# A planned attention kernel: VectorE's two PSUM banks used one by one, batches of two, half of the int16 shifts moved to GpSimd

## The chip, the cores and the metric

One core of a Trainium2 chip runs the kernel. The metric is the device time in microseconds (us). Runs are compared in the state "fast" alone; the one slow run, of `e_fill65`, is marked where its profile is used. The span is the time from the first to the last instruction in a profile, about 2 us shorter than the device time. In the profile DVE is VectorE, ACT is ScalarE, POOL is GpSimd, PE is TensorE's matmuls and PEld its weight loads.

## The reference

Two attention blocks over the same input (2048 tokens, width 512, 32 heads of 16), mixed by a gate. Block A is softmax attention and takes nearly all the time; block B is linear attention.

```python
qkv = (x @ wqkv).reshape(B, S, 3, H, Dh) ...         # S = 2048, H = 32, Dh = 16
scores = jnp.einsum("bhqd,bhkd->bhqk", q, k) * (Dh ** -0.5)
p = _softmax(scores, axis=-1)
o = jnp.einsum("bhqk,bhkd->bhqd", p, v)              # A; then @ wo
...                                                   # B: linear attention with phi
return g * a + (1 - g) * b
```

## The kernel before

The scores are 2048 *units* of 128 x 512. TensorE writes a unit into a bank of PSUM (the "S" matmuls; the tile `ps` in the profile). Each unit is exponentiated in one of two ways.

- **ScalarE**: one `Exp` for two units (two banks).
- **VectorE**: a *conversion* adds a constant to the scaled scores and writes them as int16, so that the bits read as a bf16 number are roughly an exponential. Two *shifts* add 43 and 86 to those integers. The three results, with three scalings of the values, add up to a good exponential, so such a unit costs three value ("PV") matmuls instead of one.

The whole order of work is planned in Python when the kernel is built. Where the plan leaves a gap on TensorE, and its work in the last 3413 ns of planned time is below the share `FILL`, the planner puts in *fills*: matmuls on a dummy tile (`warm`).

```python
def d_choose(start, late=0.0):                 # units for VectorE: both banks (4 and 5) or none
    if d_busy[0] or max(t_free(4), t_free(5)) > max(start + 30.0, late):
        return []
    ...
    return [(cur, j, u, 4 + k) for k, (j, u) in enumerate(got)]

def cand_op1():                                # the conversion, of two banks at once
    ...
    return C(DV, 400, 533 * n + 74, lambda: nc.vector.tensor_scalar(o, i, ZB, 0.0, op0=ALU.add, op1=ALU.max), ...)

def cand_shift():                              # a batch is four units: 2048 int16 values
    ...
    return C(DV, 300, 602, lambda: nc.vector.tensor_scalar(Z[:, z, :], Z[:, z0, :], float(m), None, op0=ALU.add), ...)

while True:                                    # the planner
    ...
    for f in (cand_s, cand_dsolo, cand_pv, cand_op1, cand_shift, cand_exp):
    ...
    fin = emit(c.E, c.dur, c.fns, c.reads, c.writes, name=c.name)
```

The softmax here doesn't subtract the row's maximum and nothing guards it: scores larger than these inputs give would overflow.

Of the kernel before, what the change touches and what calls it, by code (L numbers as in the profile page):

```python
# [14 lines left out]
STATS = {}  # L15
# [110 lines left out]
def bass_gated_mix__mha_block__linear_attn_block__prompt_kernel(  # L126
# [31 lines left out]
    FILL = 0.65  # L158
    SLK = 0.0
# [3 lines left out]
    NPS, NZ, NQZ, NVQ = 10, 8, 3, 6  # L163

    with ExitStack() as es:
# [27 lines left out]
        ones = SB([128, 2], BF16, "ones")  # L193
        dummy = SB([128, 2], FP32, "dummy")
# [5 lines left out]
        Z = SB([128, NZ, 2048], I16, "Z")  # L200
# [58 lines left out]
        r_outt = [R(f"outt{i}") for i in range(2)]  # L259
        r_gt, r_ge, r_gl, r_gnat = R("gt"), R("ge"), R("gl"), R("gnat")  # L260
# [127 lines left out]
        emit(DV, 1000, lambda: nc.vector.memset(Vc[:, 0], 1.0), writes=r_V)  # L388
        emit(PO, 150, lambda: nc.gpsimd.memset(ones[:], 1.0), writes=[r_ones])
# [36 lines left out]
        d_busy = [False]  # L426
# [71 lines left out]
        def d_batch():  # L498

            if dst["cur"] is None:  # L500
                free = [z for z in range(NZ) if not z_pend[z]]
                if len(free) < NTERM + len(dst["shifts"]) + (NTERM - 1) * dst["open"]:
                    return None
                if all(d_unit(j) is None for j in range(4)):
                    return None
                z = min(free, key=lambda q: max([0.0] + list(r_Z[q].tr.values())))
                z_pend[z] = 1
                dst["open"] += 1
                dst["cur"] = {"todo": [0, 1, 2, 3], "z": z, "units": {}, "done": 0}
            return dst["cur"]  # L510

        def d_choose(start, late=0.0):

            if d_busy[0] or max(t_free(4), t_free(5)) > max(start + 30.0, late):
                return []
            cur = d_batch()
            if cur is None:
                return []
            js = sorted(cur["todo"], key=lambda j: (head(j), -len(uq[min(head(j), NR - 1)][j])))
            got = [(j, d_unit(j)) for j in js]  # L520
            got = sorted([x for x in got if x[1] is not None][:2])
            return [(cur, j, u, 4 + k) for k, (j, u) in enumerate(got)]
# [5 lines left out]
        class C:  # L528
            __slots__ = ("E", "prio", "dur", "fns", "reads", "writes", "after", "name", "mode", "wt")

            def __init__(self, E, prio, dur, fns, reads, writes, after, name, mode=None, wt=1.0):
                self.wt = wt
                self.E, self.prio, self.dur, self.fns = E, prio, dur, fns
                self.reads, self.writes, self.after, self.name, self.mode = reads, writes, after, name, mode

        def d_loaded(extra):
            for cur, j, u, bk in extra:
                r, kb = u
                take(r, kb, j)
                cur["todo"].remove(j)  # L540
                cur["units"][j] = u
                left[r][j] += NTERM - 1
                kb_left[(r, kb)] += NTERM - 1
            if extra:
                d_busy[0] = True
                dst["op1"].append((cur, [x[1] for x in extra]))
                if not cur["todo"]:
                    dst["cur"] = None

        def cand_s():  # L550
            sset = st["set"]
            if set_busy[sset]:
                return None
            b0 = 2 * sset
            writes = [r_bank[b0], r_bank[b0 + 1]]
            start = max(PE.free, _avail(PE, [], writes))
            extra = d_choose(start, s_window()[1] - SLK)
            units = act_pick(2, {x[1] for x in extra})
            if units is None and extra:
                extra = []  # L560
                units = act_pick(2, set())
            if units is None:
                return None
            n = len(units)
            reads = s_reads(units + [(u[0], u[1], j) for _, j, u, _ in extra])
            fns = [s_fn(r, kb, j, b0 + k) for k, (r, kb, j) in enumerate(units)]
            fns += [s_fn(u[0], u[1], j, bk) for _, j, u, bk in extra]
            writes = writes[:n] + [r_bank[x[3]] for x in extra]

            def after(fin):  # L570
                for (r, kb, j) in units:
                    take(r, kb, j)
                set_busy[sset] = True
                nn = n + 10 * len(extra)
                STATS["sn"][nn] = STATS["sn"].get(nn, 0) + 1
                exps.append((sset, units))
                st["set"] = 1 - sset
                d_loaded(extra)
            STATS.setdefault('sn', {})
            return C(PE, 1000, 222, fns, reads, writes, after, f"S{units}" + "".join(f"+D{x[2]}{x[1]}" for x in extra), "row",  # L580
                     0.25 * (n + len(extra)))
# [15 lines left out]
        def cand_op1():  # L597
            if not dst["op1"]:
                return None
            cur, js = dst["op1"][0]  # L600
            z = cur["z"]
            n = len(js)

            def after(fin):
                dst["op1"].popleft()
                d_busy[0] = False
                cur["done"] += n
                d_finish(cur)
            zj = Z[:, z, :].rearrange("p (j c) -> p j c", j=4)
            o = zj[:, js[0]:js[1] + 1:js[1] - js[0], :] if n == 2 else zj[:, js[0], :]  # L610
            i = bank(4, 2).rearrange("p (j c) -> p j c", j=2) if n == 2 else bank(4)
            return C(DV, 400, 533 * n + 74, lambda: nc.vector.tensor_scalar(o, i, ZB, 0.0, op0=ALU.add, op1=ALU.max),  # L612
                     [r_bank[4 + k] for k in range(n)], [r_Z[z]], after, f"op1 {[cur['units'][j] + (j,) for j in js]}")

        def z_items(cur, z, term):
            for j, (r, kb) in cur["units"].items():
                def rel():
                    z_pend[z] -= 1
                add_item(r, kb, j, Z[:, z, 512 * j:512 * (j + 1)].bitcast(BF16), r_Z[z], rel, term, f"z{term}")

        def d_finish(cur):
            n = len(cur["units"])
            if cur["done"] < n or (cur["todo"] and any(d_unit(j) is not None for j in cur["todo"])) or cur.get("fin"):
                return
            if cur["todo"]:
                if any(head(j) < NR - 1 for j in cur["todo"]):
                    return
                dst["cur"] = None
            cur["fin"] = True
            z = cur["z"]  # L630
            dst["open"] -= 1
            z_pend[z] = n + NTERM - 1
            z_items(cur, z, 0)
            for k, m in enumerate(SHIFTS[1:]):
                dst["shifts"].append((cur, m, z, k + 1))

        def cand_shift():
# [10 lines left out]
            cur, m, z0, kt = dst["shifts"][0]  # L648

            def after(fin):  # L650
                dst["shifts"].popleft()
                z_pend[z] = len(cur["units"])
                z_pend[z0] -= 1
                z_items(cur, z, kt)
            return C(DV, 300, 602, lambda: nc.vector.tensor_scalar(Z[:, z, :], Z[:, z0, :], float(m), None, op0=ALU.add),  # L655
                     [r_Z[z0]], [r_Z[z]], after, f"shift {m}")
# [205 lines left out]
        def t_v(t8, vb):  # L862
# [12 lines left out]
            for k in range(1, NTERM):  # L875
                yield po(750, lambda k=k: nc.gpsimd.tensor_scalar(Vc[:, k, vs].rearrange("p a b c -> p (a b c)"),  # L876
# [27 lines left out]
        def aout(r):  # L904
# [27 lines left out]
            yield po(800, lambda: nc.gpsimd.tensor_tensor(t2[:, :, 16 * par:16 * par + 16], t1[:, :, 0:16],  # L932
# [7 lines left out]
        def phi(b, dst_ap, dst_res):  # L940
# [6 lines left out]
            yield po(700, lambda: nc.gpsimd.tensor_scalar(eb[:, i, :], eb[:, i, :], 1.0, 0.0, op0=ALU.min, op1=ALU.max), [r_eb[i]], [r_eb[i]])  # L947
# [260 lines left out]
        def fill_one(start, mode):  # L1208
# [19 lines left out]
            free = [7] + [b for b in owner if owner[b] is None] + ([] if d_busy[0] or 4 in owner else [5, 4])  # L1228
# [20 lines left out]
        guard = 0  # L1249
        while True:  # L1250
# [7 lines left out]
            for f in (cand_s, cand_dsolo, cand_pv, cand_op1, cand_shift, cand_exp):  # L1258
                c = f()
                if c is not None:  # L1260
                    cands.append(c)
# [6 lines left out]
            for c in cands:  # L1268
                a = _avail(c.E, c.reads, c.writes)
                start0 = start = max(c.E.free, a)  # L1270
                if c.E is PE and c.mode and c.mode != st["mode"]:
                    start = max(start, PE.free + SWITCH)
                if c.E is PE and c.prio < 1000:
# [6 lines left out]
            key, start, c = min(by.values(), key=lambda v: v[1])  # L1280
            if c.E is PE:
# [9 lines left out]
                WLOG.append(act_log[-1])  # L1291
            if isinstance(c.fns, tuple) and c.fns[0] == "DMA":
# [72 lines left out]
```

## Time and profile before

| | before |
|---|---|
| median | 740.31 us (739.58 to 740.9, 3 runs) |
| units on ScalarE / VectorE | 1460 / 588 |
| busy: PE, VectorE, ScalarE, GpSimd | 93%, 90%, 94%, 17% |

First the engine line of the page: busy us, share of the span, number of instructions. Then groups of instructions: line, engine, operation, out<-in, shapes and count; busy us and mean ns of one; idle time of the engine just before them and what ended it. L677 are the exps, L612 the conversions, L655 the shifts.

```profile
PE 689.5 (93%) x6663; PEld 209.2 (28%) x6757; DVE 667.6 (90%) x813; ACT 697.7 (94%) x769; POOL 128.3 (17%) x184
...
L677 ACT ACTIVATE P<-ps 128x1024 bf16<-128x1024 f32 x730 | 682.4, 1045 | 23.3 <-PE ps L331 22.1
L612 DVE TENSOR_SCALAR Z<-ps 128x1024 int16<-128x1024 f32 x294 | 357.2, 1215 | 42.8 <-PE ps L331 41.8
...
L655 DVE TENSOR_SCALAR Z<-Z 128x2048 int16<-128x2048 int16 x294 | 215.4, 750 | 3.0
```

Three engines are above 90%, and GpSimd is nearly idle. ScalarE's exps plus the idle time in front of them make 682.4 + 23.3 = 705.7 us (a sum) of the 740.2 us span: ScalarE sets the pace, and only fewer exps or less waiting of ScalarE can shorten the run.

The next lines are of the timeline (start us, us, engine, line, operation), the first of GpSimd, the others of VectorE, in the same stretch.

```profile
229.04 1.27 POOL L948 TENSOR_TENSOR phiK<-eb,mb 128x512 bf16<-128x512 f32 x1
```
```profile
229.34 2.11 DVE L655 TENSOR_SCALAR Z<-Z 128x2048 int16<-128x2048 int16 x2
231.38 1.21 DVE L612 TENSOR_SCALAR Z<-ps 128x1024 int16<-128x1024 f32 x1
```

Two shifts, which elsewhere take 1.3 us together, took 2.11 us here; the first started while GpSimd was in an add and ended 0.55 us after it.

### The profile page before, as it was taken

How to read it: one execution, taken by the hardware profiler on the slowest of the kernel's cores; microseconds unless marked ns; L12 is line 12 of the kernel's file. 1: busy time of each engine (PE TensorE's matmuls, PEld its weight loads, DVE VectorE, ACT ScalarE, POOL GpSimd, SP SyncE). 2: the span in 40 equal slices, each digit the busy share in tenths (PEclk: the TensorE clock that was granted, in tenths of full speed). 3: DMA queues.
4: the chain of work that ended last, by engine and by line, in shares of the span. 5: the costliest groups of instructions: out<-in, count | busy, mean ns of one | idle time of the engine just before them, and what ended most of it. 6: DMA issues, size and time to landing. Idle time of an engine off the chain costs nothing.

```text
span 740.2 us, 16623 instructions
## 1 busy us (share of the span) xinstructions
PE 689.5 (93%) x6663; PEld 209.2 (28%) x6757; DVE 667.6 (90%) x813; ACT 697.7 (94%) x769; POOL 128.3 (17%) x184
## 2 busy tenths in 40 slices
PE   6999999899999999999999999999899989999997
PEld 2322222222323222222233322222233222222222
DVE  6799999998999999988897999999999968999894
ACT  4899999999999999999999999999999969999993
POOL 1301341212311220000010034233430000000000
PEclk8999999999999999999999999999999869999999
DMA  5900000000000000000000000000002021000001
GB/s 128 317 13 15 2 5 4 2 8 2 1 8 3 8 1 2 8 2 8 1 8 3 7 3 3 7 1 3 1 8 44 19 48 30 16 15 16 16 15 36
DMA packets 27836, 15.49 MB, mean 21 GB/s; under 512 B 19696, under 2 KB 26736, under 8 KB 27760
## 3 DMA queue, kind: packets, MB, share of 16 engines
q1 hardware_dynamic: 26704, 14.17, 7.0%
q8 instruction: 53, 0.87, 0.5%
q10 hardware_dynamic: 1056, 0.26, 0.2%
q14 instruction: 23, 0.19, 0.1%
HBM read 6.69 MB, written 2.10 MB: 12 GB/s over the span
## 4 chain that ended last, share of the span: by engine, by line
PE 58%; DVE 23%; ACT 9%; issue 7%; POOL 1%; DMA 0%; ACTq 0%; POOLq 0%; DVEq 0%
PE ps L331 58%; DVE Z L612 12%; ACT P L677 9%; DVE Z L655 6%; DVE mb L945 1%; DVE T L909 1%; DVE Vc L873 1%; DMA xnat<-wA 0%; DVE QT L845 0%; DVE OAT L936 0%; DVE KT L823 0%; ACT eb L944 0%; DVE wA L1032 0%; POOL Vc L876 0%; POOL phiK L948 0%
## 5 line engine op out<-in xcount | busy, mean ns | idle before, releaser
L677 ACT ACTIVATE P<-ps 128x1024 bf16<-128x1024 f32 x730 | 682.4, 1045 | 23.3 <-PE ps L331 22.1
L612 DVE TENSOR_SCALAR Z<-ps 128x1024 int16<-128x1024 f32 x294 | 357.2, 1215 | 42.8 <-PE ps L331 41.8
L331 PE MATMUL ps<-Qz,KT 32*128 32x512 bf16 x2048 | 291.3, 390 | 15.4 <-DVE Z L612 5.2
L331 PE MATMUL ps<-Z,Vc 128*17 128x512 bf16 x1764 | 227.8, 387 | 6.9 <-DVE Z L655 6.2
L655 DVE TENSOR_SCALAR Z<-Z 128x2048 int16<-128x2048 int16 x294 | 215.4, 750 | 3.0
L331 PE MATMUL ps<-P,Vc 128*17 128x512 bf16 x1460 | 204.0, 388 | 2.7 <-ACT P L677 0.9
L331 PEld LDWEIGHTS ps<-Qz,KT 32*128 32x128 bf16 x2048 | 73.7, 91 | 259.5 <-ACT P L677 182.5
L331 PEld LDWEIGHTS ps<-Z,Vc 128*17 128x17 bf16 x1764 | 52.1, 88 | 90.3 <-issue 45.2
L331 PE MATMUL ps<-warm 128*32 128x512 bf16 (+17 forms) x524 | 70.6, 334 | 3.8 <-issue 2.2
L331 PEld LDWEIGHTS ps<-P,Vc 128*17 128x17 bf16 x1460 | 47.3, 88 | 72.5 <-issue 35.4
L929 POOL TENSOR_TENSOR rg<-rec,gt 128x16 f32<-128x16 f32 x31 | 11.8, 380 | 297.2 <-DVE rec L916 297.2
L947 POOL TENSOR_SCALAR eb<-eb 128x512 f32<-128x512 f32 x32 | 23.1, 722 | 148.9 <-DVE mb L945 74.8
L948 POOL TENSOR_TENSOR phiK<-eb,mb 128x512 bf16<-128x512 f32 x32 | 43.2, 1350 | 2.3
L876 POOL TENSOR_SCALAR Vc<-Vc 128x576 bf16<-128x576 bf16 x32 | 23.3, 727 | 88.6 <-DVE Vc L873 87.3
L331 PE MATMUL ps<-xT,wA 128*128 128x512 bf16 x105 | 33.5, 388 | 5.1 <-issue 3.1
L909 DVE STREAM_TRANSPOSE T<-ps 128x512 f32<-128x512 f32 x32 | 22.6, 707 | 9.3 <-PE ps L331 9.3
L331 PEld LDWEIGHTS ps<-warm 128*32 128x32 bf16 (+1 forms) x541 | 20.6, 95 | 23.9 <-issue 17.9
L945 DVE TENSOR_SCALAR mb<-ps 128x512 f32<-128x512 f32 x32 | 21.6, 677 | 1.3 <-PE ps L331 0.9
L331 PE MATMUL ps<-wA,xT 128*128 128x128 bf16 x256 | 21.8, 226 | 0.6 <-DVE KT L823 0.2
L944 ACT ACTIVATE eb<-ps 128x512 f32<-128x512 f32 x32 | 20.0, 624 | 0.6 <-PE ps L331 0.6
L932 POOL TENSOR_TENSOR T<-T,rg 128x256 bf16<-128x256 f32 x31 | 19.6, 632 | 2.4
L331 PE MATMUL ps<-woA,OAT 128*128 128x512 bf16 x55 | 16.6, 382 | 2.2 <-DVE OAT L924 1.2
(76 smaller groups left out, 247.0 us busy)
## 6 DMA issues: line engine op xcount, KB each, us to landing
Qz<-QT SPq DMA_DIRECT2D x120, 16.0 KB, 1.8
wA<-in_A_wqkv_dram SPq DMA_DIRECT2D x1, 1536.0 KB, 8.4
wB<-in_B_wqkv_dram SPq DMA_DIRECT2D x1, 1536.0 KB, 11.8
xnat<-in_A_x_dram SPq DMA_DIRECT2D x3, 512.0 KB, 12.7
out_dram<-outt SPq DMA_DIRECT2D x12, 128.0 KB, 1.7
xnat<-in_A_x_dram SPq DMA_DIRECT2D x4, 128.0 KB, 3.3
woA<-in_A_wo_dram SPq DMA_DIRECT2D x1, 512.0 KB, 8.7
woB<-in_B_wo_dram SPq DMA_DIRECT2D x1, 512.0 KB, 9.3
```

The costliest lines, as they stand in the source:

```text
L331: return lambda: nc.tensor.matmul(o, lhsT=l, rhs=r, start=start, stop=stop, skip_group_check=sg)
L612: return C(DV, 400, 533 * n + 74, lambda: nc.vector.tensor_scalar(o, i, ZB, 0.0, op0=ALU.add, op1=ALU.max), [r_bank[4 + k] for k in range( ...
L655: return C(DV, 300, 602, lambda: nc.vector.tensor_scalar(Z[:, z, :], Z[:, z0, :], float(m), None, op0=ALU.add), [r_Z[z0]], [r_Z[z]], after ...
L677: return C(AC, 500, 427 * n + 49, lambda: nc.scalar.activation(P[:, slot, 0:512 * n], bank(b0, n), ACT.Exp, scale=ESC), [r_bank[b0 + k] fo ...
L876: yield po(750, lambda k=k: nc.gpsimd.tensor_scalar(Vc[:, k, vs].rearrange("p a b c -> p (a b c)"), Vc[:, 0, vs].rearrange("p a b c -> p ( ...
L909: yield dv(607, lambda: nc.vector.transpose(T1[:, a, :], bank(7)), [r_bank[7]], [r_T1[a]])
L929: yield po(250, lambda: nc.gpsimd.tensor_tensor(rg[:, a, :], rec[:, a, :], gt[:, qc, :], ALU.mult), [r_rec[a], r_gt], [r_rg[a]])
L932: yield po(800, lambda: nc.gpsimd.tensor_tensor(t2[:, :, 16 * par:16 * par + 16], t1[:, :, 0:16], rg[:, a, :].unsqueeze(2).to_broadcast([1 ...
L944: yield ac(480, lambda: nc.scalar.activation(eb[:, i, :], bank(b), ACT.Exp), [r_bank[b]], [r_eb[i]])
L945: yield dv(607, lambda: nc.vector.tensor_scalar(mb[:, i, :], bank(b), 0.0, 1e-6, op0=ALU.max, op1=ALU.add), [r_bank[b], r_eb[i]], [r_mb[i]])
L947: yield po(700, lambda: nc.gpsimd.tensor_scalar(eb[:, i, :], eb[:, i, :], 1.0, 0.0, op0=ALU.min, op1=ALU.max), [r_eb[i]], [r_eb[i]])
L948: yield po(1300, lambda: nc.gpsimd.tensor_tensor(dst_ap, eb[:, i, :], mb[:, i, :], ALU.add), [r_eb[i], r_mb[i]], dst_res)
```

## The change

The intent: (1) TensorE may refill one of VectorE's two banks while the other is being converted; (2) batches of two units, so that shifts come in smaller pieces; (3) roughly half of the shifts go to the idle GpSimd, two int16 values packed in one int32 add (if the add is exact, no carry crosses from the lower value, since the sums stay below 32768). VectorE then has room for more units, which come off ScalarE. The planner also keeps a GpSimd instruction and a VectorE shift apart in its planned times (`lock`, `port`; *port* is its name for the entry that does so). The ground for it is in the trace of before: of the 45 shifts that began while a GpSimd instruction ran, 44 ended after it (by 0.55 us at the median), and the longest took 1.75 us, where a free one takes 0.685. The threshold `FILL` rises from 0.65 to 0.75 as well. The core of it, with cuts inside lines and between them shown as `...`:

```diff
-    FILL = 0.65
-    SLK = 0.0
+    FILL = 0.75
...
+    PMIN = 2
...
+    SLK = 120.0
...
-    NPS, NZ, NQZ, NVQ = 10, 8, 3, 6
+    NB = 2
+    NPS, NZ, NQZ, NVQ = 10, 16, 3, 6
...
-            if d_busy[0] or max(t_free(4), t_free(5)) > max(start + 30.0, late):
+            banks = [b for b in (4, 5) if not d_busy[b] and t_free(b) <= max(start + 30.0, late)]
+            if not banks:
                 return []
...
+            if E is PO:
+                return C(PO, 400, 200 + 532 * n, lambda: nc.gpsimd.tensor_tensor(
+                    Z[:, z, 0:512 * n].bitcast(I32), Z[:, z0, 0:512 * n].bitcast(I32),
+                    mcon[:, kt - 1:kt].to_broadcast([128, 256 * n]), ALU.add), ...)
-            return C(DV, 300, 602, lambda: nc.vector.tensor_scalar(Z[:, z, :], Z[:, z0, :], float(m), ...
+            return C(DV, 450 if hot else 300, 69 + 134 * n, lambda: nc.vector.tensor_scalar(Z[:, z, 0:512 * n], ..., lock=True)
...
+                if c.lock:
+                    start = max(start, port["pool" if c.E is DV else "dve"])
...
+            if c.lock:
+                c.E.free = max(c.E.free, start)
+                port[c.E.name] = start + c.dur + 20.0
```

Left out: bookkeeping per bank, a few priorities and planned durations of other GpSimd work.

More of the change, by code (lines that the diff above doesn't have):

```diff
@@ L157, in bass_gated_mix__mha_block__linear_attn_block__prompt_kernel @@
     SWITCH = 100.0
-    FILL = 0.65
-    SLK = 0.0
+    FILL = 0.75
+    HOT = 24
+    BACK = 600.0
+    SHB = 2
+    why = [None]
+    PMIN = 2
+    PLATE = 0.0
+    SLK = 120.0
     DSL = 300.0
     STICK = 450.0
-    NPS, NZ, NQZ, NVQ = 10, 8, 3, 6
+    NB = 2
+    NPS, NZ, NQZ, NVQ = 10, 16, 3, 6
     with ExitStack() as es:
@@ L193, in bass_gated_mix__mha_block__linear_attn_block__prompt_kernel @@
         ones = SB([128, 2], BF16, "ones")
+        mcon = SB([128, 2], I32, "mcon")
         dummy = SB([128, 2], FP32, "dummy")
@@ L199, in bass_gated_mix__mha_block__linear_attn_block__prompt_kernel @@
         P = SB([128, NPS, 1024], BF16, "P")
-        Z = SB([128, NZ, 2048], I16, "Z")
+        Z = SB([128, NZ, 512 * NB], I16, "Z")
         T1 = SB([128, 2, 512], FP32, "T1")
@@ L259, in bass_gated_mix__mha_block__linear_attn_block__prompt_kernel @@
         r_outt = [R(f"outt{i}") for i in range(2)]
+        r_mcon = R("mcon")
         r_gt, r_ge, r_gl, r_gnat = R("gt"), R("ge"), R("gl"), R("gnat")
@@ L388, in bass_gated_mix__mha_block__linear_attn_block__prompt_kernel @@
         emit(DV, 1000, lambda: nc.vector.memset(Vc[:, 0], 1.0), writes=r_V)
+        for k, m in enumerate(SHIFTS[1:]):
+            emit(PO, 150, lambda k=k, m=m: nc.gpsimd.memset(mcon[:, k:k + 1], m * 65537), writes=[r_mcon])
         emit(PO, 150, lambda: nc.gpsimd.memset(ones[:], 1.0), writes=[r_ones])
@@ L425, in bass_gated_mix__mha_block__linear_attn_block__prompt_kernel @@
         owner = {6: None}
-        d_busy = [False]
+        dcnt = [[0] * 4 for _ in range(NR)]
+        d_busy = {4: False, 5: False}
         kb_left = {(r, kb): 4 for r in range(NR) for kb in range(NKB)}
@@ L508, in d_batch @@
                 dst["open"] += 1
-                dst["cur"] = {"todo": [0, 1, 2, 3], "z": z, "units": {}, "done": 0}
+                dst["cur"] = {"todo": NB, "z": z, "units": [], "done": 0}
             return dst["cur"]
         def d_choose(start, late=0.0):
-            if d_busy[0] or max(t_free(4), t_free(5)) > max(start + 30.0, late):
+            banks = [b for b in (4, 5) if not d_busy[b] and t_free(b) <= max(start + 30.0, late)]
+            if not banks:
+                why[0] = "busy" if any(d_busy[b] for b in (4, 5)) else "late"
                 return []
@@ L517, in d_choose @@
             if cur is None:
+                why[0] = "noZ"
                 return []
-            js = sorted(cur["todo"], key=lambda j: (head(j), -len(uq[min(head(j), NR - 1)][j])))
-            got = [(j, d_unit(j)) for j in js]
-            got = sorted([x for x in got if x[1] is not None][:2])
-            return [(cur, j, u, 4 + k) for k, (j, u) in enumerate(got)]
+            got = [(j, d_unit(j)) for j in range(4)]
+            got = sorted([x for x in got if x[1] is not None], key=lambda x: (x[1][0], dcnt[x[1][0]][x[0]], -len(uq[x[1][0]][x[0]])))
+            got = sorted(got[:min(len(banks) if len(dst["op1"]) < 1 and DV.free < start + BACK and len(dst["shifts"]) < SHB else 1, cur["todo"])])
+            why[0] = "none" if not got else "ok"
+            return [(cur, j, u, b) for b, (j, u) in zip(banks, got)]
         def add_item(r, kb, j, ap, res, rel, term, name):
@@ L528, in bass_gated_mix__mha_block__linear_attn_block__prompt_kernel, with __init__ @@
         class C:
-            __slots__ = ("E", "prio", "dur", "fns", "reads", "writes", "after", "name", "mode", "wt")
-            def __init__(self, E, prio, dur, fns, reads, writes, after, name, mode=None, wt=1.0):
+            __slots__ = ("E", "prio", "dur", "fns", "reads", "writes", "after", "name", "mode", "wt", "lock")
+            def __init__(self, E, prio, dur, fns, reads, writes, after, name, mode=None, wt=1.0, lock=False):
                 self.wt = wt
+                self.lock = lock or E is PO
                 self.E, self.prio, self.dur, self.fns = E, prio, dur, fns
@@ L539, in d_loaded @@
                 take(r, kb, j)
-                cur["todo"].remove(j)
-                cur["units"][j] = u
+                cur["todo"] -= 1
+                cur["units"].append((r, kb, j))
+                dcnt[r][j] += 1
                 left[r][j] += NTERM - 1
@@ L544, in d_loaded @@
             if extra:
-                d_busy[0] = True
-                dst["op1"].append((cur, [x[1] for x in extra]))
+                for x in extra:
+                    d_busy[x[3]] = True
+                for k, x in enumerate(extra):
+                    dst["op1"].append((cur, len(cur["units"]) - len(extra) + k, [x[3]]))
                 if not cur["todo"]:
@@ L557, in cand_s @@
             extra = d_choose(start, s_window()[1] - SLK)
+            w = why[0]
             units = act_pick(2, {x[1] for x in extra})
@@ L575, in after @@
                 STATS["sn"][nn] = STATS["sn"].get(nn, 0) + 1
+                STATS.setdefault("why", {})
+                STATS["why"][w] = STATS["why"].get(w, 0) + 1
                 exps.append((sset, units))
@@ L599, in cand_op1, with z_items @@
                 return None
-            cur, js = dst["op1"][0]
+            cur, k0, bks = dst["op1"][0]
             z = cur["z"]
-            n = len(js)
+            n = len(bks)
             def after(fin):
                 dst["op1"].popleft()
-                d_busy[0] = False
+                for b in bks:
+                    d_busy[b] = False
+                z_items(cur, z, 0, range(k0, k0 + n))
+                z_pend[z] += n
                 cur["done"] += n
                 d_finish(cur)
-            zj = Z[:, z, :].rearrange("p (j c) -> p j c", j=4)
-            o = zj[:, js[0]:js[1] + 1:js[1] - js[0], :] if n == 2 else zj[:, js[0], :]
-            i = bank(4, 2).rearrange("p (j c) -> p j c", j=2) if n == 2 else bank(4)
+            o = Z[:, z, 512 * k0:512 * (k0 + n)]
+            i = bank(bks[0], n)
             return C(DV, 400, 533 * n + 74, lambda: nc.vector.tensor_scalar(o, i, ZB, 0.0, op0=ALU.add, op1=ALU.max),
-                     [r_bank[4 + k] for k in range(n)], [r_Z[z]], after, f"op1 {[cur['units'][j] + (j,) for j in js]}")
-        def z_items(cur, z, term):
-            for j, (r, kb) in cur["units"].items():
+                     [r_bank[b] for b in bks], [r_Z[z]], after, f"op1 {cur['units'][k0:k0 + n]}")
+        def z_items(cur, z, term, ks):
+            for k in ks:
+                r, kb, j = cur["units"][k]
                 def rel():
                     z_pend[z] -= 1
-                add_item(r, kb, j, Z[:, z, 512 * j:512 * (j + 1)].bitcast(BF16), r_Z[z], rel, term, f"z{term}")
+                add_item(r, kb, j, Z[:, z, 512 * k:512 * (k + 1)].bitcast(BF16), r_Z[z], rel, term, f"z{term}")
         def d_finish(cur):
             n = len(cur["units"])
-            if cur["done"] < n or (cur["todo"] and any(d_unit(j) is not None for j in cur["todo"])) or cur.get("fin"):
+            if cur["done"] < n or (cur["todo"] and any(d_unit(j) is not None for j in range(4))) or cur.get("fin"):
                 return
             if cur["todo"]:
-                if any(head(j) < NR - 1 for j in cur["todo"]):
+                if any(head(j) < NR - 1 for j in range(4)):
                     return
@@ L631, in d_finish, with cand_pshift, cand_shift @@
             dst["open"] -= 1
-            z_pend[z] = n + NTERM - 1
-            z_items(cur, z, 0)
+            z_pend[z] += NTERM - 2
             for k, m in enumerate(SHIFTS[1:]):
                 dst["shifts"].append((cur, m, z, k + 1))
-        def cand_shift():
+        def cand_pshift():
+            return cand_shift(PO)
+        def cand_shift(E=DV):
             if dst["cur"] is not None and dst["cur"]["todo"]:
@@ L648, in cand_shift @@
             cur, m, z0, kt = dst["shifts"][0]
+            n = len(cur["units"])
+            if E is PO and (len(dst["shifts"]) < PMIN or PO.free > DV.free + PLATE):
+                return None
             def after(fin):
@@ L653, in after @@
                 z_pend[z0] -= 1
-                z_items(cur, z, kt)
-            return C(DV, 300, 602, lambda: nc.vector.tensor_scalar(Z[:, z, :], Z[:, z0, :], float(m), None, op0=ALU.add),
-                     [r_Z[z0]], [r_Z[z]], after, f"shift {m}")
+                z_items(cur, z, kt, range(len(cur["units"])))
+                STATS["sh" + E.name] = STATS.get("sh" + E.name, 0) + 1
+            if E is PO:
+                return C(PO, 400, 200 + 532 * n, lambda: nc.gpsimd.tensor_tensor(
+                    Z[:, z, 0:512 * n].bitcast(I32), Z[:, z0, 0:512 * n].bitcast(I32),
+                    mcon[:, kt - 1:kt].to_broadcast([128, 256 * n]), ALU.add), [r_Z[z0], r_mcon], [r_Z[z]], after, f"pshift {m}")
+            pr = st["pv_round"]
+            hot = pr < NR and sum(left[pr]) < HOT and any(u[0] <= pr for u in cur["units"])
+            return C(DV, 450 if hot else 300, 69 + 134 * n, lambda: nc.vector.tensor_scalar(Z[:, z, 0:512 * n], Z[:, z0, 0:512 * n], float(m), None, op0=ALU.add),
+                     [r_Z[z0]], [r_Z[z]], after, f"shift {m}", lock=True)
         def cand_exp():
@@ L875, in t_v @@
             for k in range(1, NTERM):
-                yield po(750, lambda k=k: nc.gpsimd.tensor_scalar(Vc[:, k, vs].rearrange("p a b c -> p (a b c)"),
+                yield po(690, lambda k=k: nc.gpsimd.tensor_scalar(Vc[:, k, vs].rearrange("p a b c -> p (a b c)"),
                                                                   Vc[:, 0, vs].rearrange("p a b c -> p (a b c)"), COEF[k], 1.0,
@@ L931, in aout @@
             t2 = T2[:, c, :].rearrange("p (q d) -> p q d", d=32)
-            yield po(800, lambda: nc.gpsimd.tensor_tensor(t2[:, :, 16 * par:16 * par + 16], t1[:, :, 0:16],
+            yield po(640, lambda: nc.gpsimd.tensor_tensor(t2[:, :, 16 * par:16 * par + 16], t1[:, :, 0:16],
                                                           rg[:, a, :].unsqueeze(2).to_broadcast([128, 16, 16]), ALU.mult),
@@ L946, in phi @@
             yield ("FREE", b)
-            yield po(700, lambda: nc.gpsimd.tensor_scalar(eb[:, i, :], eb[:, i, :], 1.0, 0.0, op0=ALU.min, op1=ALU.max), [r_eb[i]], [r_eb[i]])
+            yield po(640, lambda: nc.gpsimd.tensor_scalar(eb[:, i, :], eb[:, i, :], 1.0, 0.0, op0=ALU.min, op1=ALU.max), [r_eb[i]], [r_eb[i]])
             yield po(1300, lambda: nc.gpsimd.tensor_tensor(dst_ap, eb[:, i, :], mb[:, i, :], ALU.add), [r_eb[i], r_mb[i]], dst_res)
@@ L1227, in fill_one @@
             t0 = PE.free + (SWITCH if m == "row" else 0.0)
-            free = [7] + [b for b in owner if owner[b] is None] + ([] if d_busy[0] or 4 in owner else [5, 4])
+            free = [7] + [b for b in owner if owner[b] is None] + [b for b in (5, 4) if b not in owner and not d_busy[b]]
             free = [b for b in free if _avail(PE, [], [r_bank[b]]) <= t0]
@@ L1249, in bass_gated_mix__mha_block__linear_attn_block__prompt_kernel @@
         guard = 0
+        port = {"pool": 0.0, "dve": 0.0}
         while True:
@@ L1257, in bass_gated_mix__mha_block__linear_attn_block__prompt_kernel @@
             cands = cand_tasks()
-            for f in (cand_s, cand_dsolo, cand_pv, cand_op1, cand_shift, cand_exp):
+            for f in (cand_s, cand_dsolo, cand_pv, cand_op1, cand_shift, cand_pshift, cand_exp):
                 c = f()
@@ L1272, in bass_gated_mix__mha_block__linear_attn_block__prompt_kernel @@
                     start = max(start, PE.free + SWITCH)
+                if c.lock:
+                    start = max(start, port["pool" if c.E is DV else "dve"])
+                    start0 = max(start0, start)
                 if c.E is PE and c.prio < 1000:
@@ L1279, in bass_gated_mix__mha_block__linear_attn_block__prompt_kernel @@
                     by[c.E] = (key, start, c)
-            key, start, c = min(by.values(), key=lambda v: v[1])
+            key, start, c = min(by.values(), key=lambda v: v[1] - (80.0 if v[2].E is DV and v[2].lock else 0.0))
             if c.E is PE:
```

## The prediction

> **What bounds the kernel now.** Three engines are nearly full: in the table of windows, from 200 to 500 us, ScalarE is busy 99%, TensorE 95%, VectorE 93%. GpSimd is busy 17% over the span. The 2048 softmax units (128 x 512 scores) are shared out: 730 ScalarE exps and 294 VectorE conversions (group L612) take two each. In the timeline fourteen exps in a row take 13.27 us, 0.474 us a unit; ScalarE's time is 1460 x 0.474 = 692 us plus 48. The span falls only if units leave ScalarE, and VectorE decides how many can. In the timeline a conversion of a pair occupies VectorE 1.14 us, a shift of four units 0.61 us: 0.875 us a unit, 514 us. Its other 226 us are other work (about 90), start and tail, waits, and shifts blocked by GpSimd (group L655: mean 750, median 685, worst 1754 ns). The list of waits gives 41.8 us of L612 on TensorE: both banks are taken and freed together, so VectorE can stand still while a new pair is written.
>
> **What changes.**
> - Conversions bank by bank: TensorE refills one bank while the other is read. A 128x512 PSUM read of the same kind takes 0.60 us back to back, instead of 0.57 a unit: about +20 us, against perhaps 25 of the 42 us of waits.
> - [...] With half on GpSimd VectorE keeps 0.17 us a unit; in all 0.77, 12% less.
> - GpSimd gets some 300 int32 adds of 512 values. The like in the trace is the phi add (L948), 1269 ns median: about 0.4 ms more, 70-75% busy. [...]
> - [...] shifts starting during a GpSimd add take up to 1754 ns. GpSimd work plus VectorE shifts must fit one after the other: about 530 + 110 us of 715. It fits, tightly; conversions from PSUM can run beside GpSimd. I allow 15 us more blocking.
> - TensorE: about 55 more VectorE units are 110 more value matmuls, four at a time, some 6 us, plus more warm-up fills. No new bound, but little slack.
>
> **The sum.** ScalarE: (2048 - n) x 0.474 + 48. VectorE: n x 0.77 + 218 (226, less 25 of waits, plus 15 blocking, plus 2). Equal at n = 643: 714 us. The order of work is fixed beforehand and more engines now depend on each other: I add 3 us. Nearly all of the gain is on the critical path; some 30 us at start and tail stay.
>
> Prediction: 717 us (3.1% less), 8 in 10 between 698 and 735. Faster by over 2%: 0.68; within 2%: 0.26; slower: 0.06.
>
> **What would show it.** Exps fall from 730 to about 703, ScalarE still 98-99% busy in the middle; about 640 one-bank conversions; 300-340 VectorE shifts of 0.34-0.45 us; GpSimd 70-75% busy, adds of about 1.27 us; L612's wait on TensorE below 20 us.
>
> **What would make it wrong.** The port: if VectorE's shifts (mean far over 0.45 us) or the GpSimd adds stretch waiting for one another, the gain is eaten and the time stays at 735 or more. TensorE: if single-bank loads cost extra passes, or fills delay real work, ScalarE idles. If GpSimd's late terms hold up value matmuls, buffers run out. In the other direction, if nearly all waits vanish, 700 us.

The 0.17 us a unit rests on that estimate, so the sum can't be followed in full from what is printed: with 0.17, and so 0.77, taken as they stand it came to 714 us, and with the 3 us added to 717. The estimate was the author's; in the changed kernel free shifts of 1024 values start every 0.336 us in a row, and half of that is 0.17. What the other steps rest on in the trace of before: that GpSimd's work and the shifts must fit one after the other, on the 44 of 45 shifts above; that conversions can run beside GpSimd, on 79 of the 294 that overlap its instructions, of which the longest took 1225 ns, and of the others 1226; the 6 us of TensorE, on value matmuls in a row, four of which take 0.22 us (median, start to start).

## More of the kernel before

The runs were made in several sessions on different chips, each beside the kernel before, which had a median of 740.2 to 741.8 us in them; so times of two sessions are compared to about 2 us. The granted clock is the share of full clock that the profiler saw TensorE get.

The planner keeps for each engine the time when it is free, takes durations from written constants, picks the instruction that can start first, and emits it. What comes out is one fixed instruction stream per engine, with semaphore waits **only where data or buffers require them**. The planned times themselves are not in the program.

## The result, and the profile after

The changed kernel takes 748.56 us (748.27 to 752.29, 4 runs) against 740.21 us for before (4 runs). The ratio is 1.0124, 95% interval 1.0091 to 1.0157: within 2%, but on the slow side. (A ratio here is the mean time of one kernel's fast runs over that of the other's of the same rounds, so it is not quite the ratio of the medians.) The prediction of 717 us was wrong.

The same parts of the page of the changed kernel. L716 are the exps, L637 the conversions, L689 the GpSimd adds, L694 the VectorE shifts.

```profile
PE 685.4 (92%) x6934; PEld 211.8 (28%) x7026; DVE 672.6 (90%) x1131; ACT 691.2 (93%) x754; POOL 464.0 (62%) x519
...
L716 ACT ACTIVATE P<-ps 128x1024 bf16<-128x1024 f32 x715 | 675.7, 1037 | 36.1 <-PE ps L340 33.5
L637 DVE TENSOR_SCALAR Z<-ps 128x512 int16<-128x512 f32 x619 | 414.1, 682 | 48.7 <-PE ps L340 34.9
L689 POOL TENSOR_TENSOR Z<-Z,mcon 128x512 int32<-128x512 int32 x333 | 350.3, 1075 | 151.8 <-DVE Z L637 113.6
...
L694 DVE TENSOR_SCALAR Z<-Z 128x1024 int16<-128x1024 int16 (+1 forms) x287 | 168.4, 622 | 0.3
```

The work was moved as intended: 619 units on VectorE instead of 588, 333 of 620 shifts on GpSimd, 15 fewer exps. But the busy time of ScalarE's exps fell by only 6.7 us while the waiting before them rose by 12.8 us. Together these are +6.1 us, all of the span's difference (746.4 - 740.2 = 6.2). ScalarE waits for TensorE, so the next question is what TensorE waits for. From the lists of waits (engine, its line, the one waited for: us in total, times, longest us), first before, then after:

```profile
PEld ps L331 <- DVE Z L655: 30.1, 93, 1.5
...
ACT P L677 <- PE ps L331: 22.1, 39, 3.2
...
PE ps L331 <- DVE Z L655: 6.9, 19, 1.2
PE ps L331 <- DVE Z L612: 6.7, 21, 0.9
```
```profile
PEld ps L340 <- DVE Z L694: 34.9, 84, 1.3
ACT P L716 <- PE ps L340: 33.5, 64, 1.6
...
PE ps L340 <- DVE Z L694: 14.5, 30, 1.0
...
PE ps L340 <- DVE Z L637: 14.2, 46, 1.1
```

TensorE's matmuls wait twice as long for VectorE's shifts and conversions (6.9 + 6.7 us before, 14.5 + 14.2 after), though a shift is now half as large. The reason stands in the shifts' own durations (min/median/max):

```profile
L694 DVE TENSOR_SCALAR Z<-Z x287: 284/420/1498, 12.4 to 730.0; 128x1024 int16<-128x1024 int16 x143, 128x512 int16<-128x512 int16 x1
```

The median is 0.42 us but the mean is 0.622. The conversions, which read PSUM, show nothing of the kind:

```profile
L637 DVE TENSOR_SCALAR Z<-ps x619: 619/684/694, 10.8 to 727.8; 128x512 int16<-128x512 f32 x155
```

456 of the 619 overlap GpSimd instructions, and the longest took 694 ns. In the timeline near 305 us, VectorE first and then GpSimd:

```profile
304.94 3.11 DVE L694 TENSOR_SCALAR Z<-Z 128x1024 int16<-128x1024 int16 x4
307.97 0.68 DVE L884 TENSOR_SCALAR QT<-ps 128x512 bf16<-128x512 f32 x1
```
```profile
305.10 2.33 POOL L689 TENSOR_TENSOR Z<-Z,mcon 128x512 int32<-128x512 int32 x2 [3.17 <-DVE Z L637]
```

Four shifts took 3.11 us. Free shifts in a row start every 0.34 us and last about 0.42 us, so four would take an estimated 1.4 us. Here they took turns with the two adds: the second and the third shift lasted 1.26 us each, started while an add ran and ended 0.28 us after it, and the adds took 1.15 and 1.22 us instead of 1.04. For each kernel I summed, from the trace, the duration of every shift that overlaps a GpSimd instruction, less the median of the shifts that overlap none. I call this **blocking**. It is 19.5 us before (75 of 294 shifts) and 59.6 us after (153 of 287; free median 0.415 us).

### The profile page after: what moved, and what is told of

It reads as the page before. It is cut to its first block, busy times and chain, and to the rows that moved or that the text cites. A ratio compares the mean times of both kernels' runs of the same rounds, so it can differ in the third digit from the quotient of the medians.

```text
span 746.4 us, 18462 instructions
## 1 busy us (share of the span) xinstructions
PE 685.4 (92%) x6934; PEld 211.8 (28%) x7026; DVE 672.6 (90%) x1131; ACT 691.2 (93%) x754; POOL 464.0 (62%) x519
## 4 chain that ended last, share of the span: by engine, by line
PE 52%; DVE 30%; issue 9%; ACT 6%; POOL 1%; DMA 1%; DVEq 0%; ACTq 0%; POOLq 0%
PE ps L340 52%; DVE Z L637 17%; DVE Z L694 9%; ACT P L716 6%; POOL Z L689 1%; DVE mb L984 1%; DVE T L948 1%; DMA xnat<-wA 1%; DVE QT L884 0%; DVE OAT L975 0%; DVE Vc L912 0%; DVE KT L862 0%; ACT eb L983 0%; DVE wA L1071 0%; DVE gnat L940 0%
## 5 line engine op out<-in xcount | busy, mean ns | idle before, releaser
L716 ACT ACTIVATE P<-ps 128x1024 bf16<-128x1024 f32 x715 | 675.7, 1037 | 36.1 <-PE ps L340 33.5
L637 DVE TENSOR_SCALAR Z<-ps 128x512 int16<-128x512 f32 x619 | 414.1, 682 | 48.7 <-PE ps L340 34.9
L689 POOL TENSOR_TENSOR Z<-Z,mcon 128x512 int32<-128x512 int32 x333 | 350.3, 1075 | 151.8 <-DVE Z L637 113.6
L340 PE MATMUL ps<-Qz,KT 32*128 32x512 bf16 x2048 | 281.7, 388 | 19.5 <-DVE Z L637 7.9
L340 PE MATMUL ps<-Z,Vc 128*17 128x512 bf16 x1857 | 272.3, 385 | 11.8 <-DVE Z L694 8.7
L340 PE MATMUL ps<-P,Vc 128*17 128x512 bf16 x1429 | 247.8, 386 | 7.2 <-DVE Z L694 4.6
L694 DVE TENSOR_SCALAR Z<-Z 128x1024 int16<-128x1024 int16 (+1 forms) x287 | 168.4, 622 | 0.3
L340 PEld LDWEIGHTS ps<-Z,Vc 128*17 128x17 bf16 x1857 | 63.0, 88 | 103.9 <-issue 39.7
L340 PE MATMUL ps<-warm 128*32 128x512 bf16 (+17 forms) x736 | 76.5, 319 | 3.6 <-POOL warm L382 1.4
L340 PEld LDWEIGHTS ps<-P,Vc 128*17 128x17 bf16 x1429 | 58.0, 88 | 75.0 <-issue 34.4
L968 POOL TENSOR_TENSOR rg<-rec,gt 128x16 f32<-128x16 f32 x31 | 7.0, 224 | 37.0 <-DVE rec L955 36.1
```

The source lines that it names most:

```text
L340: return lambda: nc.tensor.matmul(o, lhsT=l, rhs=r, start=start, stop=stop, skip_group_check=sg)
L689: return C(PO, 400, 200 + 532 * n, lambda: nc.gpsimd.tensor_tensor(Z[:, z, 0:512 * n].bitcast(I32), Z[:, z0, 0:512 * n].bitcast(I32), mcon ...
L694: return C(DV, 450 if hot else 300, 69 + 134 * n, lambda: nc.vector.tensor_scalar(Z[:, z, 0:512 * n], Z[:, z0, 0:512 * n], float(m), None, ...
L716: return C(AC, 500, 427 * n + 49, lambda: nc.scalar.activation(P[:, slot, 0:512 * n], bank(b0, n), ACT.Exp, scale=ESC), [r_bank[b0 + k] fo ...
```

## The experiments

Theories at the start. **Port**: VectorE's shifts stand still behind GpSimd's adds; as the streams are in order, everything on VectorE behind them is late (in the timeline above the next instruction starts only after the fourth shift, at 307.97 us), TensorE waits, ScalarE idles. **Bank**: single-bank conversions cost more per unit (0.64 us of VectorE's time against 0.585 before, each counted until the next VectorE instruction starts), and the port is a side show. **TensorE**: the extra fills (748 weight loads for them against 541) delay real work. Inside the port theory there was a second question: *why* do they collide, when the planner keeps them apart? Its add costs 1.264 us and the chip's 1.04, so a **wrong cost** was the first suspect.

All runs had 3 rounds, beside the kernel before. "Blocking" as defined above; ScalarE idle is that before exps, from the group line.

| run | median us (range) | ratio to before (95%) | blocking us | ScalarE idle us |
|---|---|---|---|---|
| after (given) | 748.56 (748.27-752.29) | 1.0124 (1.0091-1.0157) | 59.6 | 36.1 |
| e_short_add | 721.21 (719.29-723.84) | 0.9726 (0.9691-0.9762) | 17.9 | 15.3 |
| e_no_port | 712.48 (710.27-715.96) | 0.9622 (0.9584-0.9660) | 2.1 | 9.3 |
| e_dve_shifts | 737.23 (733.85-741.13) | 0.9942 (0.9897-0.9987) | 15.0 | 19.5 |
| e_pair | 758.56 (755.16-762.05) | 1.0228 (1.0187-1.0269) | 46.5 | 40.1 |
| e_add_cost | 747.92 (743.0-752.28) | 1.0090 (1.0027-1.0153) | 52.3 | 41.7 |
| e_fill65 | 759.33 (758.71-764.08) fast, 770.92 slow | 1.0260 (1.0221-1.0299) | 60.2 (slow profile) | 56.3 (slow profile) |
| e_order | 711.47 (709.47-715.4) | 0.9603 (0.9569-0.9637) | 3.7 | 7.9 |
| e_order_cost | 708.29 (705.78-710.41) | 0.9552 (0.9523-0.9581) | 12.0 | 9.0 |
| e_dve_order | 728.02 (726.76-731.83) | 0.9844 (0.9808-0.9880) | 3.3 | 9.7 |
| e_pair_order | 727.25 (724.61-732.66) | 0.9834 (0.9785-0.9884) | 7.9 | 11.1 |
| e_order_fill65 | 718.74 (716.11-719.79) | 0.9698 (0.9663-0.9733) | 5.1 | 15.9 |
| e_before_order | 743.94 (737.83-745.85) | 1.0036 (0.9985-1.0087) | 20.0 | 24.5 |

### Is it the port? Short adds, then shifts of another shape

`e_short_add` keeps every instruction and its order and lets an add occupy GpSimd only briefly (0.24 us in the trace, where a full one takes 1.04). Its results are wrong on purpose, and were flagged as wrong.

```diff
+                w = 64 if STATS.get("shpool", 0) >= 30 else 512 * n
-                    Z[:, z, 0:512 * n].bitcast(I32), Z[:, z0, 0:512 * n].bitcast(I32),
-                    mcon[:, kt - 1:kt].to_broadcast([128, 256 * n]), ALU.add)
+                    Z[:, z, 0:w].bitcast(I32), Z[:, z0, 0:w].bitcast(I32),
+                    mcon[:, kt - 1:kt].to_broadcast([128, w // 2]), ALU.add)
```

> Wrong results on purpose: same instruction order as the changed kernel, but from the 31st on the GpSimd adds cover 32 instead of 512 packed values[...]. Port theory (VectorE's shifts stand still behind adds: 153 of 287 shifts overlap GpSimd work and cost about 60 us over the free median of 0.415 us): shift mean falls from 0.62 to below 0.46 us, ScalarE's idle time shrinks by 10 us or more, time 725 to 737 us. Bank theory (single-bank conversions cost 0.635 instead of 0.585 us a unit) and TensorE theory (more fills, more passes): shifts may get shorter, the time stays at 744 to 750 us.

It took 721.21 us, 27 us less than the changed kernel and a little below the range that the port theory gave. Blocking fell to 17.9 us; most of the rest is at shifts that meet the other GpSimd work, little of it at the first full adds or the short adds alone. But short adds also deliver their values earlier, so this run alone does not separate the port from late values.

`e_no_port` does. GpSimd's adds stay full. VectorE's shift is given another shape: it covers 510 of the 1024 values, read as 3 rows of 170 and written as one row of 510. That a shift of this shape would not be held up by GpSimd no earlier run had shown; the run tests it.

```diff
+            so, si = Z[:, z, 0:512 * n], Z[:, z0, 0:512 * n]
+            if n == 2 and STATS.get("shpool", 0) + STATS.get("shdve", 0) >= 40:
+                so, si = Z[:, z, 0:510], Z[:, z0, 0:516].rearrange("p (a b) -> p a b", a=3)[:, :, 0:170]
-            ... nc.vector.tensor_scalar(Z[:, z, 0:512 * n], Z[:, z0, 0:512 * n], float(m), None, op0=ALU.add)
+            ... nc.vector.tensor_scalar(so, si, float(m), None, op0=ALU.add)
```

> Wrong results on purpose: the changed kernel in its own order with full GpSimd adds (1.04 us), but from the 41st shift on VectorE's shift covers 510 of 1024 values, read as three rows and written as one[...]. Port theory: shifts no longer stand still behind adds, mean under 0.45 us with adds still overlapping them, time 718 to 732 us like the run with short adds. Late-add theory (short adds helped because their values came sooner): time 742 to 750 us although the shifts run free.

The groups of that run:

```profile
L719 ACT ACTIVATE P<-ps 128x1024 bf16<-128x1024 f32 x715 | 666.0, 1055 | 9.3 <-PE ps L340 8.8
L637 DVE TENSOR_SCALAR Z<-ps 128x512 int16<-128x512 f32 x619 | 418.3, 685 | 62.0 <-PE ps L340 47.0
L689 POOL TENSOR_TENSOR Z<-Z,mcon 128x512 int32<-128x512 int32 x333 | 338.1, 1039 | 129.1 <-DVE Z L637 102.2
...
L697 DVE TENSOR_SCALAR Z<-Z 128x510 int16<-128x510 int16 (+2 forms) x287 | 108.9, 416 | 0.3
```

The adds are full ones (1039 ns), 190 of the 287 shifts overlap GpSimd work, and yet a shift takes 416 ns, as long as a free one. (It covers half the values but is no shorter: in a row they start every 0.325 us, full shifts every 0.336.) The profile shows that the shifts no longer wait; it does not show why this shape escapes. The time is 712.48 us, below the range that I had given. Late values are ruled out as the main cause. So are the bank theory and the TensorE theory: the same conversions and the same fills in the same order are there. (The run passed the comparison with the reference although half of each such shift is stale. So that comparison is not sharp for the shifted terms, and it does not by itself prove the int32 add exact.)

### Which part of the change is it?

`e_dve_shifts` drops the GpSimd part; `e_pair` keeps it and drops the one-by-one use of the banks (with 14 buffers, as the planner got stuck with 16).

```diff
-            for f in (cand_s, cand_dsolo, cand_pv, cand_op1, cand_shift, cand_pshift, cand_exp):
+            for f in (cand_s, cand_dsolo, cand_pv, cand_op1, cand_shift, cand_exp):      # e_dve_shifts
```
```diff
-            if not banks:
+            if len(banks) < 2:                                                            # e_pair
-                for k, x in enumerate(extra):
-                    dst["op1"].append((cur, len(cur["units"]) - len(extra) + k, [x[3]]))
+                dst["op1"].append((cur, len(cur["units"]) - len(extra), [x[3] for x in extra]))
```

> The change without its GpSimd part: all shifts on VectorE, banks one by one, batches of two. VectorE then needs about 0.63 + 0.34 = 0.97 us a unit, against 0.93 before. Port theory: shifts at 0.42 us mean with under 20 us of blocking; time 742 to 758 us, so GpSimd's adds in the changed kernel bring only a few us net. Bank theory: the loss is here already, time 752 us or more, clearly above the changed kernel's 748. If it came out under 738 us the GpSimd adds would be harmful outright.

> GpSimd adds and batches of two kept, but both banks taken and converted together as before (14 buffers of Z, as the planner cannot finish with 16); the plan has 185 or so adds on GpSimd and 400 shifts on VectorE, 562 units off ScalarE. Bank theory: conversions back at 0.585 us a unit, time 725 to 737 us. Port theory: shifts still collide with adds and VectorE waits for TensorE again (30 us or more), time 742 to 756 us.

Without GpSimd adds the kernel took 737.23 us, slightly less than before (ratio 0.9942, interval 0.9897 to 0.9987) and clearly less than the full change. I had expected them to be worth a few us; the branch that I had written down as "harmful outright" is the one that came. With the adds but with paired banks it took 758.56 us, just above the port theory's range and nowhere near the bank theory's. So the loss came with the adds, and not with banks one by one. How much the banks alone are worth without order, `e_pair` can't say: its plan also has 14 buffers, 174 adds instead of 333, and a lower granted clock (0.966 to 0.975, against 0.979 to 0.989 in the changed kernel).

### Fills

`e_fill65` puts one constant back (`FILL = 0.65`).

> The changed kernel with the threshold of warm-up fills put back from 0.75 to 0.65 (230 fill groups planned instead of 262, 229 before). TensorE theory: fills delay real work, time 738 to 744 us and ScalarE idle down by 5 us or more. Port theory: no difference, 745 to 752 us.

Its fast runs took 759.33 us, slower rather than faster. The TensorE theory falls. That it is 11 us slower than the changed kernel, with the same blocking in its one (slow) profile, fits neither theory as I had written it.

One rival stood outside both theories: the granted clock. In the fast runs of `e_fill65` it was 0.969 to 0.983, in the changed kernel 0.979 to 0.989. Among the four runs of one kernel, 0.01 of clock goes with some 4 to 8 us (`e_add_cost`: 752.28 us at 0.956, 743.0 at 0.976; `e_order`: 715.4 at 0.985, 709.47 at 0.994). So the lower clock may stand for an estimated 5 of the 11 us (at 5 us for 0.01); no run varied it alone. It is not what made the change fail: the changed kernel had a higher clock than most runs of the kernel before (0.971 to 0.990), and `e_order` below gains 37 us with 0.985 to 0.994, of which the clock may stand for an estimated 2 us.

### Why do they collide? Wrong cost or missing wait

`e_add_cost` corrects the planner's number, nothing else: `C(PO, 400, 500 * n, ...)` for `200 + 532 * n`.

> One number of the planner: it reckons an add of two units at 1.00 us (measured back to back 0.997) instead of 1.264, so it gives GpSimd 413 and VectorE 227 shifts and moves 637 units off ScalarE. Wrong-cost theory (the planned order keeps shifts and adds apart, but the chip's adds are 0.26 us shorter, so GpSimd runs ahead of the plan and collides): blocking of shifts falls from 60 to under 35 us, time 725 to 737 us. Port theory without that: the two engines drift for other reasons, blocking stays above 45 us, time 738 to 750 us.

Blocking stayed at 52.3 us, although there are fewer shifts (227, not 287), and the time at 747.92 us. By the blocking, the wrong cost is not the cause. (The time alone is a weaker witness: this kernel ran at a clock of 0.956 to 0.976, which at its own 4.6 us for 0.01 may hide an estimated 11 us of gain.) `e_order` leaves the wrong cost and makes the plan binding: each GpSimd instruction also waits for the VectorE shift that was planned just before it. No arithmetic, no order and no buffer changes.

```diff
-        def emit(E, dur, fns, reads=(), writes=(), name=""):
+        def emit(E, dur, fns, reads=(), writes=(), name="", extra=()):
...
-            deps = deps_of(E, reads, writes)
+            deps = deps_of(E, reads, writes) + list(extra)
...
+        lastsh = [None]
...
-                fin = emit(c.E, c.dur, c.fns, c.reads, c.writes, name=c.name)
+                fin = emit(c.E, c.dur, c.fns, c.reads, c.writes, name=c.name, extra=[e for e in [lastsh[0]] if e is not None and c.E is PO])
+                if c.lock and c.E is DV:
+                    lastsh[0] = _Ev(DV, DV.n)
```

> The changed kernel in its own order, right results; the only edit: each GpSimd instruction also waits for the VectorE shift that the plan put before it, so GpSimd can't run ahead of the plan and take the port first. Drift theory (collisions come from GpSimd starting earlier than planned, its adds being 1.04 us and not 1.264): blocking of shifts falls from 60 to under 30 us, time 728 to 742 us. If the collisions come from VectorE's shifts starting early or late instead, blocking stays above 45 us and the time 745 us or more.

> As the ordered run, and the planner reckons an add at 1.04 us instead of 1.264 (391 adds, 243 VectorE shifts, 633 units off ScalarE). Drift theory: blocking under 30 us and more units moved, 722 to 738 us, better than the ordered run alone. Against: above 742 us.

The result is right and takes 711.47 us, below the range that I had given and 37 us less than the changed kernel. Its groups:

```profile
L716 ACT ACTIVATE P<-ps 128x1024 bf16<-128x1024 f32 x715 | 665.5, 1054 | 7.9 <-PE ps L340 7.5
L637 DVE TENSOR_SCALAR Z<-ps 128x512 int16<-128x512 f32 x619 | 417.8, 684 | 58.8 <-PE ps L340 44.1
L689 POOL TENSOR_TENSOR Z<-Z,mcon 128x512 int32<-128x512 int32 x333 | 338.3, 1038 | 159.5 <-DVE Z L694 98.8
...
L694 DVE TENSOR_SCALAR Z<-Z 128x1024 int16<-128x1024 int16 (+1 forms) x287 | 112.9, 430 | 0.3
```

The same 287 shifts take 112.9 us instead of 168.4. The wait has moved to GpSimd (98.8 us of the idle time before its adds now end with a shift), which is only 64% busy and has time for it. From the waits of this run:

```profile
PEld ps L340 <- DVE Z L694: 11.6, 47, 0.4
```

TensorE's waits for shifts fell from 34.9 + 14.5 us to this and 0.5 us. ScalarE's exps and the idle time before them fell by (675.7 + 36.1) - (665.5 + 7.9) = 38.4 us, which is nearly the span's 746.4 - 707.7 = 38.7. Some 10 us of it are in the busy column, though the 715 exps are the same: in the ordered run exps in a row start every 0.90 us and last 1.05, so they overlap, and the column counts overlapped time once. So a part of the waiting can hide in "busy". The windows (us busy, x instructions: PE, PEld, DVE, ACT, POOL; clock; DMA share; GB/s), first after, then with the wait:

```profile
200.00:400.00 200.00, 186.11 (x1922) 56.39 (x1944) 184.82 (x308) 192.60 (x209) 130.61 (x141) 1.00 0.02 5
```
```profile
200.00:400.00 200.00, 197.75 (x2081) 59.27 (x2079) 178.99 (x330) 199.98 (x220) 129.95 (x145) 1.00 0.02 5
```

In the middle of the run ScalarE goes from 96% to 99.99% busy, with VectorE *less* busy and doing more (330 instructions instead of 308). There ScalarE alone is the limit. And `e_no_port`, which removes the blocking in another way from the same order of work, comes to the same time within about 1 us (712.48 and 711.47).

Laying the plan beside the trace shows why. Of the changed kernel's 116 shifts that were held up (over 0.48 us and overlapping GpSimd work), 107 met a GpSimd instruction that the plan had placed *after* them and that had begun before them; those account for 57.9 us. With the corrected cost alone the figures are 78 of 93 and 46.6 us. With the wait there are none. GpSimd, released by nothing but its data (the conversion), ran ahead of the plan and began first. Why the two engines leave the planned times even with the corrected cost was not taken apart.

With the corrected cost as well, `e_order_cost` took 708.29 us, below its range and the lowest of all, ratio 0.9552. The step from `e_order` is 3 us and the two intervals overlap, so that the corrected cost helps here is not shown; blocking was 12.0 us, all of it behind GpSimd instructions planned before the shifts.

### With order kept, what is each part worth?

The same wait was added to the two partial versions, to the lower fill threshold, and to the kernel before.

> The change without GpSimd adds (737 us unordered, 15 us blocking), with the one wait. Theory: 726 to 735 us, so that with order kept the adds are worth 15 to 25 us (ordered changed kernel 711). Rival, that the adds themselves are worth nothing and the order is everything: 708 to 716 us.

> Both banks converted together, GpSimd adds, with the one wait (unordered 758 us, 46 us blocking). Theory: blocking under 10 us, 725 to 738 us; above the ordered changed kernel's 711 by what banks one by one are worth. If 716 us or less, banks one by one bring nothing.

> The ordered changed kernel with the fill threshold 0.65. Unordered, 0.65 came out at 762 us against 748 with the same 60 us of blocking. If fills themselves matter, 722 us or more here; if 762 was another unlucky order meeting the same collisions, 707 to 716 us.

> The kernel before, its own order, with the one wait: each GpSimd instruction also waits for the VectorE shift put before it. Before, 75 of 294 shifts overlap GpSimd work and lose about 19 us. Removing 57 us of such blocking in the changed kernel brought 37 us of time, about 0.65 us each; so if half to all of the 19 us goes, 728 to 736 us. If before has enough slack to hide it, or its GpSimd results now come too late, 738 us or more.

- Without GpSimd adds 728.02 us, with paired banks 727.25, with both parts 711.47. Each half of the change (the adds; the banks one by one) is worth about 16 us once order is kept; both expectations held.
- The lower fill threshold took 718.74 us, between my two branches. So 7 us of `e_fill65`'s excess over the changed kernel remain with order kept, by the fewer fills and their clock (0.985 to 0.993, an estimated 2 to 3 us) or by the different order that they lead to; which stays open. The wait itself took off 41 us (759.33 to 718.74).
- The kernel before got nothing (743.94 us, ratio 1.0036, interval across 1). I had expected 728 to 736. Blocking stayed at 20.0 us: its planner knows no port, so its plan itself places shifts inside GpSimd instructions. All 35 shifts that were held up in this run (over 0.745 us, where a free one takes 0.685) met only instructions planned before them. The wait enforces a plan; it can't mend one.

## Why the prediction was wrong

- **Bound, right.** The exps and the waits before them make up 95% of the span before and after, and their change is the change of the span in both comparisons.
- **Work moved, nearly.** 715 exps (703 predicted), 619 conversions (640), 287 VectorE shifts (300 to 340). GpSimd was 62% busy, not 70-75%; an int32 add took 1.04 us, not 1.27.
- **VectorE's cost of a unit, missed.** Predicted: 12% less. From the busy columns: before (357.2 + 215.4) / 588 = 0.974 us, after (414.1 + 168.4) / 619 = 0.941, 3% less. With the wait (417.8 + 112.9) / 619 = 0.857, 12% less. The shifts are the whole difference: 0.182 us a unit with the wait, where the prediction said 0.17, and 0.272 without.
- **The step that failed: "I allow 15 us more blocking."** The mechanism was named (and listed as what could make the prediction wrong), but the term was mis-sized: blocking rose by 40 us (19.5 to 59.6). The term was also put in the wrong place. With 40 instead of 15 my sum still gives only 723 us (n = 624), because there blocking costs VectorE alone, and ScalarE keeps its fixed 48 us beside the exps. In the fixed streams a late shift made TensorE wait and then ScalarE: with 1429 units at 0.474 us, 677 us, these "48" came to 71 us in the changed kernel and to 34 in the ordered one. I had reasoned that GpSimd's work and VectorE's shifts fit one after the other in the span. They do fit, as the ordered run shows at 711 us. (That this is close to the 714 of my sum is in part luck: only 619 units left ScalarE and not 643, for which the sum gives 725 us, and ScalarE's other time was 34 us and not 48.) But nothing in the program makes them go one after the other. The planner's `port` is a bookkeeping entry at build time; the streams have no wait between a shift and an add that touch different buffers.
- **Who begins first, not asked.** In the trace of the changed kernel what began first held the other up. All 126 shifts that began while a GpSimd instruction ran ended after it, by 0.28 to 0.39 us (the two of 1.26 us above by 0.28). The 76 adds that began while a shift ran took 1.09 to 1.30 us, those that overlap no shift 1.03 to 1.04. I used this only to add up durations, and not to ask who would begin first.
- **L612's waits, missed and beside the point.** I expected VectorE's wait for TensorE below 20 us; it was 34.9 after and 44.1 in the faster ordered run. In that run ScalarE was 99.99% busy in the middle, so VectorE's idle time cost nothing there.

## What to carry to other kernels

This is one kernel's lesson. When two engines hold each other up, as the shifts and the GpSimd adds did here, and no data dependency expresses it, a planned order is only a hope: put the order into semaphores, and let the engine with slack wait for the one without. Before moving work to an idle engine, look in a trace for what its instructions hold up and for who is in the queue behind that; the price is the number of collisions times what is left of the instruction that began first (here 116 held-up shifts lost 0.51 us each, half an add), and what it costs in time depends on who waits for the blocked engine. A wait that is added can be worth more than a cost that is corrected: here one wait was worth 37 us, and the corrected cost without it brought nothing that shows.
